# Bucketed attention with a squared-ReLU block: the operand sums of the second part are issued at other places, and three more pairs add their last key block on VectorE

## Chip, core and metric

The kernel runs on one core of one Trainium2 chip. The metric is the device time of one execution in microseconds (us). A core has TensorE (PE; its weight loads are the row PEld), VectorE (DVE), ScalarE (ACT), GpSimd (POOL) and SyncE (SP). Each of them works through its own queue of instructions in order, and SP, ACT and POOL also issue DMAs from theirs.

## What is computed

First, hash attention over 4 batches of 8 heads, with 768 positions and 64 features a head. A query sees the keys whose six sign bits under a random projection are the same as its own:

```python
q_bits = (np.einsum('bhsd,dk->bhsk', q, proj) > 0).astype(np.int64)
k_bits = (np.einsum('bhsd,dk->bhsk', k, proj) > 0).astype(np.int64)
...
mask = q_bucket[:, :, :, None] == k_bucket[:, :, None, :]
scores = np.where(mask, scale * np.matmul(q, k.transpose(0, 1, 3, 2)), -1000000000.0)
...
attn = attn / (np.sum(attn, axis=-1, keepdims=True) + 1e-09)
return np.matmul(attn, v).astype(np.float32)
```

Its output, heads side by side, is x of 3072 tokens by 512 features. The second part is `h = x @ w_in; r = np.maximum(h, 0.0); out = (r * r) @ w_out`, with w_in 512 x 2048 and w_out 2048 x 512. The two weights arrive as 64-bit floats, and the kernel makes 32-bit floats of them.

## The kernel before

**Attention** goes over 16 pairs of heads (`for pr in range(NP)`, L598), four pairs a batch. A pair has six key blocks of 128 keys. `score` (L394, L411) makes the products of a key block on PE and their exponentials on ACT (tile `e`). `attend` (L436) multiplies them by the values into `xo`. The sum of the exponentials over the keys has two steps. `add_up` (L421, L426) adds up the key blocks on DVE into the tile `total`. Then `sum_up` (L455) adds over the 128 partitions on PE, with a matmul by a matrix of ones, into the PSUM tile `tot`. In the pairs named in the dictionary `sums` (L533), `add_up` leaves the sixth key block out, and `sum_up` makes a second round of matmuls that adds it straight from `e` (L450: `srcs = [totals[pr]] + [weights[pr, SB - 1]] * (pr in sums)`). After the matmuls, DVE transposes `tot` (`flip`, L461), takes the reciprocal (`once`, L463) and writes `both` (L467). PE spreads that (`spread`, L478), and DVE normalizes (`normalize`, L488 and L494). SP stores the result to `x_all` in device memory (L498).

The order of the work is written out by hand (`tc.manual_schedule()`), and each engine gets its instructions in the order of the program. A pair's own end, `finish(pr - 1)`, is issued within the next pair, after its first two key blocks. In a pair, DVE also transposes q and k of the next pair (`features`, L331) and rounds two blocks of 64-bit weights (`part_weight`, L141 and L145; `round_weight`, L169, L174, L177). SP loads them (L128) and stores the rounded ones (L188).

**The second part** replaces eight products of blocks by seven (`product`, L697), which takes sums of the operands. It goes over 3 chunks of 1024 tokens. In a chunk, `hidden(i, r)` makes eight units of 256 hidden columns each; then `project(i)` multiplies by w_out, which is split in the same way twice. A unit of `hidden` takes the operands in this order: `x` (its four blocks b11, b12, b21 and b22 lie in one tile `x`) for two products, then `t2`, `t1`, `t3`, then `x` again, and last `t4`, which is b12 rewritten. Three pieces of work prepare this beside the attention:

- `sums_in(c)`, for each of four quarters of the columns of w_in: four DVE instructions (L508 to L511, tiles `s_in`) and eight DMAs on SP (L201) to `w_in_7`. Quarter 3 belongs to the units 6 and 7.
- `load_x(0)`, one DMA on POOL's queue (L542), and `load_unit(0)` and `load_unit(1)` on SP's (L552).
- `sums_x(0, n)`: four subtractions of 128x1024 on DVE (L514), which give t1, t3, t2 and b12 of the first chunk. For the later chunks the same four are made within `project`, after its products k = 3 and k = 4.

In the kernel before, `NIN` is 8, `PB` is 4 and `X_0` is 9. So `sums` holds the pairs 4, 5, 8 and 9 (`sums_in` of the quarters 0 to 3) and the pairs 10 and 11 (the two halves of `sums_x`). In those six pairs PE adds the last key block, and in the other ten DVE does. `load_x(0)` stands at the start of pair 9, and the two `load_unit` in pair 10. The last pair, 15, has no next pair, and so no `features`.

After the loop come `finish(15)`, `normalize(15)` and the rounding of the last block of weights; then `hidden(0, 0)` begins.

Of the kernel before, what the change touches and what calls it, by code (L numbers as in the profile page):

```python
# [34 lines left out]
def kernel(  # L35
# [22 lines left out]
    NP = B * H // 2  # L58
    PB = H // 2
# [42 lines left out]
    def turn(name):  # L102

        return ps_s.tile([P, 2, 512], FP32, name=name, tag="turn")
# [4 lines left out]
    NIN = 2 * NFT  # L109
# [267 lines left out]
    def weigh(pr):  # L377

        t = bits[pr, 1]
        nc.scalar.activation(out=t, in_=t, func=ACTF.Copy, scale=gains)  # L380
# [65 lines left out]
    def sum_up(pr, tot):  # L446


        tot = tot[:, 0]
        srcs = [totals[pr]] + [weights[pr, SB - 1]] * (pr in sums)  # L450
        for src in srcs:
            for c in range(2):
                for h in range(2):
                    g = 2 * h + c
                    nc.tensor.matmul(  # L455
                        out=tot[g * 32:(g + 1) * 32, 0:HS], lhsT=ones,
                        rhs=src[:, h, c * HS:(c + 1) * HS],
                        start=src is srcs[0], stop=src is srcs[-1],
                    )
        flip = p_n.tile([P, HS], FP32, name="flip")  # L460
        nc.vector.transpose(out=flip, in_=tot[:, 0:HS])  # L461
        once = p_n.tile([P, NB], FP32, name="once")
        nc.vector.reciprocal(  # L463
            out=once, in_=flip.rearrange("p (n f) -> p n f", f=32)[:, :, 0]
        )
        both = p_n.tile([P, 2, NB], FP32, name="both")
        nc.vector.tensor_tensor(  # L467
            out=both, in0=which,
            in1=once.rearrange("p (o n) -> p o n", o=1).to_broadcast([P, 2, NB]), op=ALU.mult,
        )  # L470
        onces[pr] = both
# [12 lines left out]
    def normalize(pr):  # L484
        b, j = divmod(pr, PB)
        rec = recs.pop(pr)
        over = p_n.tile([P, S], FP32, name="recs")
        nc.vector.transpose(  # L488
            out=over.rearrange("p (n f) -> p n f", f=32),
            in_=rec.rearrange("p (n o) -> p n o", o=1).to_broadcast([P, S // 32, 32]),  # L490
        )
        x_t = p_x.tile([P, S], FP32, name="x_t")
        xo = outs.pop(pr)
        nc.vector.scalar_tensor_tensor(  # L494
            out=x_t, in0=xo[:, 0:S], scalar=xo[:, S:S + 1],
            in1=over, op0=ALU.add, op1=ALU.mult,
        )
        nc.sync.dma_start(out=x_all[:, j, b * S:(b + 1) * S], in_=x_t)  # L498
# [14 lines left out]
    def minus(out, in0, in1):  # L513
        nc.vector.tensor_tensor(out=out, in0=in0, in1=in1, op=ALU.subtract)  # L514
# [14 lines left out]

    X_0 = 2 * PB + 1
    sums = {c // 2 * (NIN // 2) + c % 2 + NIN // 2: (sums_in, c) for c in range(4)}  # L533
    for n in range(2):
        sums[X_0 + 1 + n] = lambda n: sums_x(0, n), n

    xs = {}

    def load_x(i):

        x = p_c.tile([P, NFT, NCH], FP32, name="x")
        nc.gpsimd.dma_start(out=x, in_=x_all[:, :, i * NCH:(i + 1) * NCH])  # L542
        xs[i] = x, [p_c.tile([P, 2, NCH // 2], FP32, name=f"t_x{n}") for n in range(3)]
# [7 lines left out]
            w_unit[n] = pool.tile([P, 7, NFT // 2, P], FP32, name="w_unit", bufs=2 if pool is p_i else 1)  # L551
            nc.sync.dma_start(out=w_unit[n], in_=w_in_7[r])  # L552

    def sums_x(i, n):

        x, (t1, t2, t3) = xs[i]
        lo, hi = slice(0, NCH // 2), slice(NCH // 2, NCH)
        b11, b12, b21, b22 = x[:, 0:2, lo], x[:, 0:2, hi], x[:, 2:4, lo], x[:, 2:4, hi]
        if n == 0:
            minus(t1, b12, b11)  # L560
            minus(t3, b22, b12)
        else:
            minus(t2, b22, t1)
            minus(b12, b21, t2)

    def finish(pr, beside=None):

        tot = turn("tot")
        if beside:
            beside()  # L570
        sum_up(pr, tot)
        for kt in (SB - 2, SB - 1):
            attend(pr, kt)
        spread(pr)

    with tc.manual_schedule():
# [21 lines left out]
        for pr in range(NP):  # L598
            a, b = 2 * pr, 2 * pr + 1
            more = pr + 1 < NP  # L600

            def prepare():

                hash_bits(pr + 1, turn("hash"))
                for w in (1, 0):
                    signs(pr + 1, w)


            if pr + 2 < NP:
                load_pair(pr + 2)  # L610
            if pr == X_0:
                load_x(0)
            if more and pr > 0:
                for w in range(2):
                    features(pr + 1, w)
            if pr > 0:
                round_weight(b - 2)
                load_weight(b)
            score(pr, 0)
            if pr == 0:  # L620
                first_keys(1, turn("hash"))
            score(pr, 1)
            if pr > 0:
                finish(pr - 1, prepare if more else None)
            add_up(pr, 1)
            if pr == 0:
                for w in range(2):
                    features(1, w)
            if pr > 0:
                normalize(pr - 1)  # L630


            if pr == X_0 + 1:
                for n in range(2):
                    load_unit(n)
            part_weight(a)
            score(pr, 2)
            score(pr, 3)
            if pr == 0:
                prepare()  # L640
            elif more:
                weigh(pr + 1)
            place_power(a)
            attend(pr, 0)
            attend(pr, 1)
            for kt in (2, 3):
                add_up(pr, kt)
            if more:
                load_values(pr + 1)


            round_weight(a)
            part_weight(b)
            if more:
                load_weight(a + 2)
            score(pr, 4)
            score(pr, 5)
            if pr == 0:
                weigh(1)
            place_power(b)  # L660
            attend(pr, 2)
            attend(pr, 3)
            add_up(pr, 4)

            if pr not in sums:
                add_up(pr, 5)
            if pr in sums:
                f, n = sums[pr]
                f(n)
        finish(NP - 1)  # L670
        normalize(NP - 1)
        round_weight(2 * NP - 1)
        first.close()

# [9 lines left out]
        b11, b12, b21, b22, b_t = (  # L684
            p_g.tile([P, NR, HN], FP32, name=f"b{n}") for n in ("11", "12", "21", "22", "_t")
        )
# [196 lines left out]
        def project(i):  # L883
# [59 lines left out]
            for k in range(7):  # L943
                b = OUTER[k][1]
                t1, t2 = tens.pop(k)
                at = lambda m, k=k: lambda n: leaves[k, m][:, n]
                bt = {
                    "11": lambda n: b[:, n, 0:QN], "21": lambda n: b[:, NQ + n, 0:QN],
                    "22": lambda n: b[:, NQ + n, QN:HN], "t1": lambda n: t1[:, n],
                    "t2": lambda n: t2[:, n], "t3": lambda n: b[:, n, QN:HN],  # L950
                    "t4": lambda n: b[:, NQ + n, 0:QN],
                }

                def hook():
                    y21 = b[:, NQ:NR, 0:QN]
                    minus(y21, y21, t2)
                    if k + 1 < 7 and k not in (1, 3):
                        inner_sums(k + 1)

                counted = []  # L960

                def a_with_load(m, k=k):
                    load_leaf(7 * k + len(counted) + NLEAF - 2)
                    counted.append(m)
                    return at(m)

                use = uses[k]
                product(
                    NQ, QN, a_with_load, bt, lambda *p: use(0, *p), lambda *p: use(1, *p),
                    lambda p: use(2, p, None), lambda *p: use(3, *p), hook,  # L970
                )
                if k == 0 and i + 1 < NCHUNK:
                    load_x(i + 1)
                if k in (3, 4) and i + 1 < NCHUNK:
                    sums_x(i + 1, k - 3)
                if k == 5 and i + 1 == NCHUNK:
                    guard()
                if k == 0:

                    for h in range(2):  # L980
                        at_h = slice(h * NQ, (h + 1) * NQ)
                        minus(b11[:, at_h], b22[:, at_h], b_t[:, at_h])
                    inner_sums(2)
                if k == 2:

                    for h in range(2):
                        at_h = slice(h * NQ, (h + 1) * NQ)
                        minus(b_t[:, at_h], b21[:, at_h], b11[:, at_h])
                    inner_sums(4)
# [309 lines left out]
```

## Time and profile before

| | |
|---|---|
| median of 5 runs | 890.98 us (890.34 to 892.87) |
| the profiled execution | 891.22 us, of which the span of the profile is 889.4 us |
| busy, of the span | PE 876.3 us (99%), DVE 711.0 us (80%), ACT 376.5 us (42%), POOL 91.7 us (10%) |
| attention | to 336.4 us; the rest is the second part |
| granted clock of TensorE | 1.00 in every stage looked at |

The profile has several views. The page gives each engine's busy time, the costliest groups of instructions and, by shares, the chain of work that ended last, followed back from the last instruction. The trace answers more closely. It lists that chain piece by piece in order of time (start, length, engine, tile, line); the instructions of one engine in order of time (start, length, line, operation, output<-inputs, and in brackets how long the engine sat idle before it and what ended that); and a table of busy times by stretches of time. A group such as "L455 tot<-e x48" counts records: an fp32 matmul leaves two of them, so 48 records are 24 matmuls of six pairs.

### The profile page before, as it was taken

The page shows a single profiled execution, that of the slowest core. Times are in us where ns is not written, and L with a number is a line of the kernel's source. Part 1 is how long each engine was busy: PE and PEld are TensorE (multiplying, and loading weights), DVE is VectorE, ACT ScalarE, POOL GpSimd, SP SyncE. Part 2 cuts the span into 40 slices and gives each one's busy share as a digit, 9 for nine tenths or more (in the row PEclk, how much of TensorE's full clock was granted, in tenths as well). Part 3 has the DMA queues.
Part 4 walks back from the last instruction along what each step waited for, and adds up shares of the span by engine and source line. Part 5 has one row for each costly group of instructions (what it writes and reads, how often), then busy time and mean ns, then how long its engine had stood idle before and what let it go on. Part 6 is the DMA issues. An engine that isn't in the chain of part 4 may idle for free.

```text
span 889.4 us, 11762 instructions
## 1 busy us (share of the span) xinstructions
PE 876.3 (99%) x4292; PEld 503.2 (57%) x4292; DVE 711.0 (80%) x991; ACT 376.5 (42%) x609; POOL 91.7 (10%) x148
## 2 busy tenths in 40 slices
PE   8999999999999999999999999999999999999996
PEld 4444444444444444444688854445888644458885
DVE  5899999999999986888779955568789556778875
ACT  5988888888888851222111112222111122221110
POOL 2000000000000000554000111112000111100002
PEclk9999999999999999999999999999999999999998
DMA  9678779899976325999855743447756444444565
GB/s 186 122 150 134 196 184 191 178 276 217 266 160 148 119 90 211 292 267 286 314 174 154 190 87 125 141 154 257 253 163 171 79 154 153 150 134 144 164 174 101
DMA packets 220032, 158.14 MB, mean 178 GB/s; under 512 B 163808, under 2 KB 180704, under 8 KB 219968
## 3 DMA queue, kind: packets, MB, share of 16 engines
q1 hardware_dynamic: 186848, 84.04, 38.8%
q10 hardware_dynamic: 22384, 37.76, 13.9%
q0 software_dynamic: 10736, 35.53, 13.2%
q8 instruction: 35, 0.57, 0.3%
q14 instruction: 29, 0.24, 0.1%
HBM read 119.28 MB, written 38.01 MB: 177 GB/s over the span
## 4 chain that ended last, share of the span: by engine, by line
PE 95%; DVE 3%; ACT 1%; issue 0%; DVEq 0%
PE acc L697 59%; PE st L394 17%; PE xo L436 14%; PE tot L455 2%; PE hash L344 1%; DVE total L426 1%; ACT bits L354 1%; PE xo L324 0%; ACT e L411 0%; DVE peaks L738 0%; DVE b L787 0%; DVE h L786 0%; PE tp L307 0%; DVE t L514 0%; PE xo L478 0%
## 5 line engine op out<-in xcount | busy, mean ns | idle before, releaser
L697 PE MATMUL acc<-x,w_unit 128*128 128x512 f32 x384 | 169.3, 592 | 0.0
L411 ACT ACTIVATE e<-st 128x1024 f32<-128x1024 f32 x192 | 145.1, 810 | 48.7 <-PE st L394 44.3
L394 PE MATMUL st<-feat,feat 64*128 64x512 f32 (+1 forms) x768 | 150.4, 483 | 0.0
L436 PE MATMUL xo<-e,v_nat 128*64 128x512 f32 (+1 forms) x768 | 134.8, 492 | 0.0
L697 PE MATMUL acc<-b,leaf 128*128 128x256 f32 x600 | 132.9, 379 | 0.0
L697 PE MATMUL acc<-t_x,w_unit 128*128 128x512 f32 x288 | 127.6, 592 | 0.0
L697 PEld LDWEIGHTS acc<-x,w_unit 128*128 128x128 f32 x384 | 72.9, 190 | 90.5 <-issue 88.0
L697 PEld LDWEIGHTS acc<-b,leaf 128*128 128x128 f32 x600 | 114.0, 190 | 16.8 <-issue 1.4
L426 DVE TENSOR_TENSOR total<-total,e 128x1536 f32<-128x1536 f32 x58 | 101.9, 1757 | 3.8
L436 PEld LDWEIGHTS xo<-e,v_nat 128*64 128x64 f32 x768 | 51.4, 136 | 82.4 <-issue 75.6
L697 PEld LDWEIGHTS acc<-t_x,w_unit 128*128 128x128 f32 x288 | 54.6, 190 | 69.0 <-issue 66.7
L394 PEld LDWEIGHTS st<-feat,feat 64*128 64x128 f32 x768 | 66.0, 188 | 33.9 <-issue 24.8
L786 DVE TENSOR_TENSOR h<-acc,two 128x512 f32<-128x512 f32 x24 | 16.6, 691 | 85.2 <-PE acc L697 85.1
L704 ACT COPY two<-acc 128x512 f32<-128x512 f32 (+1 forms) x45 | 21.9, 487 | 132.6 <-PE acc L697 129.5
L697 PE MATMUL acc<-t,leaf 128*128 128x256 f32 x336 | 76.5, 380 | 0.3 <-DVE t L514 0.3
L354 ACT ACTIVATE bits<-hash,lifts 32x384 bf16<-32x384 f32 x120 | 68.8, 573 | 3.2 <-issue 1.3
L697 PEld LDWEIGHTS acc<-t,leaf 128*128 128x128 f32 x336 | 63.6, 190 | 9.8 <-DVE t L514 1.1
L704 ACT COPY one<-acc 128x512 f32<-128x512 f32 (+1 forms) x45 | 21.9, 487 | 111.0 <-PE acc L697 77.6
L787 DVE SCALAR_TENSOR_TENSOR b<-h 128x512 f32<-128x512 f32 x96 | 64.3, 690 | 2.5
L394 PE MATMUL st<-bits,bits 64*128 64x256 bf16 (+1 forms) x384 | 63.0, 325 | 1.8 <-ACT e L411 1.4
L697 PE MATMUL acc<-b_t,leaf 128*128 128x256 f32 x240 | 53.8, 379 | 0.0
L697 PEld LDWEIGHTS acc<-b_t,leaf 128*128 128x128 f32 x240 | 45.5, 190 | 6.2
(130 smaller groups left out, 870.1 us busy)
## 6 DMA issues: line engine op xcount, KB each, us to landing
leaf<-w_out ACTq DMA_DIRECT2D x142, 256.0 KB, 3.0
w_unit<-w_in SPq DMA_DIRECT2D x24, 896.0 KB, 4.7
raw<-in_moe_w_in_dram SPq DMA_DIRECT2D x16, 512.0 KB, 5.5
raw<-in_moe_w_out_dram SPq DMA_DIRECT2D x16, 512.0 KB, 4.3
w_out<-sums POOLq DMA_DIRECT2D x16, 448.0 KB, 6.8
v_nat<-in_v_dram SPq DMA_DIRECT2D x16, 384.0 KB, 4.3
x_all<-x_t SPq DMA_DIRECT2D x16, 384.0 KB, 3.1
x<-x_all POOLq DMA_DIRECT2D x3, 2048.0 KB, 11.8
```

What stands on the lines that cost most here:

```text
L344: nc.tensor.matmul(out=banks[g * NR_B:(g + 1) * NR_B, h, 0:HS], lhsT=projs[rows], rhs=feat[pr, w][rows, c * HS:(c + 1) * HS], start=True, ...
L354: nc.scalar.activation(out=t[h * D:h * D + NR_B, c * HS:(c + 1) * HS], in_=hashed[pr, w][at, h, 0:HS], func=ACTF.Sign, scale=HUGE, bias=li ...
L394: nc.tensor.matmul(out=st[:, h, 0:hi - lo], lhsT=src[pr, 1][rows, key], rhs=src[pr, 0][rows, lo:hi], start=first, stop=not first,)
L411: nc.scalar.activation(out=e[:, :, lo:hi], in_=sts[i][:, :, 0:hi - lo], func=ACTF.Exp, scale=scale)
L426: nc.vector.tensor_tensor(out=totals[pr], in0=totals[pr], in1=weights[pr, kt][:, :, 0:S], op=ALU.add)
L436: nc.tensor.matmul(out=xo[h * D:(h + 1) * D, lo:hi], lhsT=nat[pr, "v_nat"][:, h, kt * D:(kt + 1) * D], rhs=weights[pr, kt][:, h, lo:hi], s ...
L455: nc.tensor.matmul(out=tot[g * 32:(g + 1) * 32, 0:HS], lhsT=ones, rhs=src[:, h, c * HS:(c + 1) * HS], start=src is srcs[0], stop=src is sr ...
L697: nc.tensor.matmul(out=acc[to], lhsT=a(i), rhs=b(i), start=first and i == 0, stop=last and i == n - 1, skip_group_check=True,)
L704: nc.scalar.copy(out=t, in_=acc[of])
L786: nc.vector.tensor_tensor(out=h, in0=one, in1=two, op=ALU.add)
L787: nc.vector.scalar_tensor_tensor(out=out[:, r], in0=h, scalar=0.0, in1=h, op0=ALU.max, op1=ALU.mult)
```

## The change

`sums` becomes pairs 4, 5 and 8 (quarters 0, 1 and 2), so 13 pairs have their last key block added on DVE instead of ten. `X_0` becomes 12: `load_x(0)` is issued at the start of pair 12 and the two `load_unit` in pair 13. `sums_in(3)` is issued at the start of pair 15, ahead of the rounding of weights there. The four subtractions of the first chunk are single calls now, and are issued after the loop: t1 ahead of `finish(15)`, t2 and t3 within it after `sum_up`, and b12 after `normalize(15)`. Within `project` they are made in the order t1, t2, then t3, b12.

```diff
-    X_0 = 2 * PB + 1
-    sums = {c // 2 * (NIN // 2) + c % 2 + NIN // 2: (sums_in, c) for c in range(4)}
-    for n in range(2):
-        sums[X_0 + 1 + n] = lambda n: sums_x(0, n), n
+    X_0 = 3 * PB
+    sums = {NIN // 2: 0, NIN // 2 + 1: 1, NIN: 2}
...
-    def sums_x(i, n):
+    def sum_x(i, n):
...
-        if n == 0:
-            minus(t1, b12, b11)
-            minus(t3, b22, b12)
-        else:
-            minus(t2, b22, t1)
-            minus(b12, b21, t2)
+        minus(*((t1, b12, b11), (t2, b22, t1), (t3, b22, b12), (b12, b21, t2))[n - 1])
...
         sum_up(pr, tot)
+        if pr == NP - 1:
+            sum_x(0, 2)
+            sum_x(0, 3)
         for kt in (SB - 2, SB - 1):
...
                 load_x(0)
+            if not more:
+                sums_in(3)
             if more and pr > 0:
...
             if pr in sums:
-                f, n = sums[pr]
-                f(n)
+                sums_in(sums[pr])
+        sum_x(0, 1)
         finish(NP - 1)
         normalize(NP - 1)
+        sum_x(0, 4)
         round_weight(2 * NP - 1)
...
                 if k in (3, 4) and i + 1 < NCHUNK:
-                    sums_x(i + 1, k - 3)
+                    sum_x(i + 1, 2 * k - 5)
+                    sum_x(i + 1, 2 * k - 4)
```

## The prediction

> **What bounds the kernel now.** I read the page's shares first: PE is busy 99% of the span, DVE 80%. A busy PE is no proof, since its ends are modelled, so next comes the chain that ended last, piece by piece. From 30 us to the last pair it runs on PE alone, with no gap. These are pieces of it (start, length, engine, tile, line, count):
>
> ```profile
> 236.54 1.43 PE tot L455 x16
> ...
> 257.09 1.43 PE tot L455 x16
> ...
> 277.65 0.78 PE tot L455 x8
> ...
> 331.03 1.77 DVE total L426
> 332.80 0.04 issue
> 332.84 0.85 PE tot L455 x8
> 333.70 2.74 PE xo L436 x16
> 336.44 0.08 PE xo L478 x4
> ```
>
> Two things are to be seen. In pairs that stand in `sums`, the matmuls of `tot` take 1.43 us of the path, in the others 0.78. And in the last pair the chain goes over DVE: PE waits for `total`. The table of stretches, one from each `tot` to the next, gives the pitch (stretch, its length, PE busy, PEld, DVE, ACT, POOL, clock, DMA share, GB/s):
>
> ```profile
> 236.54:257.09 20.55, 20.55 (x160) 9.39 (x164) 19.07 (x23) 17.08 (x26) 0.00 (x0) 1.00 0.83 176
> 277.65:297.55 19.90, 19.90 (x152) 9.15 (x156) 18.55 (x23) 17.07 (x26) 0.00 (x0) 1.00 0.49 133
> ```
>
> PE fills both. DVE has 18.55 us of work in a pair that adds all six blocks and 19.07 in one with half of `sums_x`. Last, DVE's instructions in order of time, for the quarter sums of pair 8 and the start of pair 15:
>
> ```profile
> 190.04 0.68 DVE L508 TENSOR_TENSOR s_in<-in 128x512 f32<-128x512 f32 x1
> ...
> 192.57 0.97 DVE L331 STREAM_TRANSPOSE feat<-q_nat 128x768 f32<-128x768 f32 x1
> ...
> 313.93 0.68 DVE L169 SCALAR_TENSOR_TENSOR power<-raw,power 128x512 uint32<-128x512 uint32 x1
> 314.53 0.68 DVE L174 SCALAR_TENSOR_TENSOR top<-raw,top 128x512 f32<-128x512 uint32 x1
> 315.25 0.69 DVE L177 SCALAR_TENSOR_TENSOR out_piece<-top,power 128x512 f32<-128x512 f32 x1
> 317.50 0.58 DVE L461 STREAM_TRANSPOSE flip<-tot 128x384 f32<-128x384 f32 x1 [1.56 <-PE tot L455]
> ```
>
> Four quarter sums take 192.57 - 190.04 = 2.53 us, and in pair 15 DVE has 1.56 us free before it must transpose `tot`.
>
> **Pairs 9, 10 and 11: the second round of `tot` goes.** It costs 1.43 - 0.78 = 0.65 us of PE, which the pitches confirm (20.55 - 19.90). PE is the whole path there: 3 x 0.65 = **1.95 us less**. DVE gains three additions of 1.76 us and loses the quarter sums (2.53) and four subtractions (two take 2.27 us from start to start, 231.14 to 233.41). It ends each pair with less work than before, the work of pairs 12 and 13, which run at 19.90 with 0.65 us of DVE idle ahead of `flip`. If that cover went, PE would wait for `total`; but a plain `total` is done at 274.1 and wanted at 277.65. ACT's work is unchanged.
>
> The Trainium skill, TensorEngine Tiling (Array Packing), section Tiling Modes, says that a change of the tiling mode drains TensorE. The first round keeps that change, so the rule has the second round cost less than half, and the rows agree (0.65 against 0.78). Without it one might take half of 1.43, which would make 2.15 us of saving instead of 1.95.
>
> **`load_x`, `load_unit`.** POOL has no other work between 20 and 350 us, and `load_x(0)` sat 179 us there, until a store of pair 7's x landed. It should start as before, at 184.8 us, since it waits for data and not for its place; if it moves to pair 12 instead, its 12 us of transfer end some 50 us ahead of t1. Two `load_unit` (1.3 us of SP) move to pair 13, where SP is idle for 5 us at a time, and land about 45 us ahead of use. Both cost nothing.
>
> **Pair 15: `sums_in(3)`.** Its 2.53 us stand ahead of the weight rounding. Back to back, L177 lasts 0.61 us to the next start, so `flip` can start at 315.25 + 0.61 + 2.53 = 318.39 and not at 317.50: 0.89 us late. PE's `spread` needs `both` 0.96 us after the start of `flip`, at 319.4; it is issued at 319.79, so PE does not wait there. But from `recs` at 320.30 to the end of `total` at 332.80 DVE runs without a gap worth naming (the chain is on it), so `total` ends 0.9 us late, and PE, which waited 0.43 us for it, waits 1.3. **0.9 us more.** The ends are nothing (DVE's late start is taken up somewhere) and 2.53 (none of the idle time is usable); I take the worked value, since instruction after instruction starts back to back in that stretch.
>
> Its eight DMAs took 5.7 and 4.2 us of SP in pairs 8 and 9. In pair 15 the store of block 29 and the load of block 31 (315.97 and 316.35) queue behind them, and the load leaves by about 320.9. With the 4.3 us such a load takes it lands by 325.2, and DVE wants it at 328.5 + 0.9. Without that margin of 4 us, each us late is one on the path.
>
> **The tail.** Times are those of before, plus the 0.9 of the last pair. `total` ends at 333.7; t1 takes DVE to 334.9, `flip` follows, so `both` is there at 336.0, and PE wants it at 337.0. Then t2 and t3 (337.2 and 338.4), the two of `normalize` (340.4), b12 (341.6), and the rounding (343.6). `hidden(0, 0)` starts on PE at 337.35; a product takes 1.72 us there (four records at 0.43). So t2 is wanted at 340.9, t1 at 342.6, t3 at 344.3, b12 at 347.6: margins of 3.7 us or more, and each would cost only what it is late. Behind the later rounding stand DVE's first output of `hidden` (341.3, now 343.6), hidden by the 5.26 us for which DVE then idled, and on SP the loads of w_out rows, 2 us later against PE. Those reach DVE just as it wants them (351.8 against 351.9). If they are later, DVE slips, has 3.05 us of idle in unit 2, and PE waits for none of it. Nothing.
>
> The longer wait in the last pair leaves the clock alone if the 0.43 us of idle there, at a granted clock of 1.00, is a guide. The Trainium skill, TensorE: Matmul & The Clock Gate, Part 1, gives an idle window of about 3.4 us for the halving of the clock, and 1.3 us is under that, so by it too nothing is added; no row here shows the halving.
>
> The order within `project` changes no instruction; PE is busy throughout there. **Sum: -1.95 + 0.9 = -1.05 us.** From the profiled 891.22 that is 890.17; the median of before lies 0.24 under its profiled run, so 889.93, or **889.9 us**.
>
> **Rivals.** (1) *The whole saving stays.* The 0.9 us are absorbed in pair 15 (another of its waits gives way): 890.98 - 1.95 = 889.0. For it speaks that DVE idled 1.56 us; against it, that the chain shows DVE as last through that pair.
>
> (2) *Slower: the first product of `hidden` waits for the last write of `x`.* b12 is rewritten in the tile `x` after `normalize`, and the first matmuls of the second part read other blocks of the same tile. If waits are kept by tile, PE starts at 341.6 and not at 337.35: 4.25 us more, 890.98 - 1.05 + 4.25 = 894.2. It decides as soon as b12 ends after 337.35, so it would decide. Against it speak PE's and DVE's rows at the start of `project`:
>
> ```profile
> 432.68 1.67 PE L697 MATMUL acc<-b,leaf 128*128 128x256 f32 x7
> ...
> 435.90 0.42 DVE L514 TENSOR_TENSOR b<-b 128x256 f32<-128x256 f32 x1
> ```
>
> The DVE instruction rewrites one half of a block of b11 and stands earlier in the program; PE reads the other half 3.2 us before it runs. So waits are kept by region, there in one row of the tile, here over two rows, which the trace does not show. By the page on the clock such an idle time of over 4 us would come on top with a slower clock.
>
> (3) *Little or no gain.* DVE becomes the bound in pairs 9 to 11, or block 31 comes late by about a us: the 1.95 are eaten in part or whole, and the 0.9 stay: 890.8 to 891.9. Against it, pairs 12 and 13 already do this work at 19.90 us.
>
> **Numbers.** Forecast 58% (its own range 889.2 to 890.6), rival 1 20% (888.5 to 889.5), rival 3 12%, rival 2 10%. The range from 888.7 to 891.4 holds the forecast, most of rival 1 and over half of rival 3, some 82%. A difference of 0.2%, about what a measurement of this kernel can tell from no change, is 1.78 us: faster means under 889.2, slower over 892.8. Three quarters of rival 1 and a tenth of the forecast make faster 0.21; rival 2 and a little of rival 3 make slower 0.11; the rest is 0.68.
>
> **What would show it.** `tot` of 0.78 us and a pitch of 19.90 in the stretches after pairs 9, 10 and 11; `flip` in pair 15 without idle time before it; PE's wait for `total` at 1.3 us; the first matmul of `hidden` right behind `spread`. Wrong if PE idles anywhere between `spread` and the second unit, if DVE waits for block 31, or if `total` of pair 15 ends no later against PE than before.

## The result and the profile after

The changed kernel takes 889.43 us (median of 29 runs, 888.99 to 891.97), the kernel before 890.97 (52 runs). The ratio is 0.9983, with a 95% interval from 0.9978 to 0.9988: 1.5 us less, between 1.1 and 2.0. The forecast was 1.05 less, 889.9, and the range held the time.

The chain of work that ended last, of the changed kernel (start, length, engine, tile, line, count):

```profile
215.37 0.78 PE tot L455 x8
...
235.28 0.78 PE tot L455 x8
...
255.19 0.78 PE tot L455 x8
...
309.70 1.76 DVE total L426
311.46 0.61 DVE s_in L508
...
312.09 1.82 DMA w_in<-s_in
...
315.23 0.69 DVE out_piece L177
315.92 0.50 DVE flip L461
...
330.91 0.85 PE tot L455 x8
...
334.50 0.08 PE xo L478 x4
```

The three `tot` of pairs 9 to 11 are at 0.78. The pairs follow one another at 19.91, as the plain pairs do; the table of stretches shows it from the `tot` of `finish(10)`, and from that of `finish(12)`, to the next one:

```profile
235.28:255.19 19.91, 19.91 (x152) 9.16 (x156) 18.58 (x23) 17.07 (x26) 0.00 (x0) 1.00 0.72 157
275.10:295.00 19.90, 19.90 (x152) 9.13 (x156) 18.55 (x23) 17.07 (x26) 0.00 (x0) 1.00 0.68 218
```

The second is a stretch whose work on PE and DVE the change did not touch, and the first now looks like it, in DVE's work too (18.58 us against 18.55). The chain now leaves PE already at the end of pair 14: it is on DVE from 309.70 us (`total` of pair 14, then `s_in`) to `total` of pair 15. Before, it was on PE until 320.28 us. (One piece there is named after the store of a sum; DVE's own order in that stretch has no gap, as the next rows show.)

Two profiled runs can't simply be subtracted: already the `tot` of pair 8 starts at 194.75 us and not at 195.37. Up to there the two programs do the same work. The offset is there from the first 10 us on: PE's transposes of the first k, which in the later run wait for a load (0.39 us), start at 7.00 us before and at 6.43 now, and the first `tot` at 34.88 and 34.27. So it seems to come from the first loads, which land at another time in each run. In the experiments this `tot` starts at 194.93 to 195.33 where nothing ahead of it differs. So everything below is read from one **stretch**: from the start of the first `tot` matmul of pair 8's finish to the first matmul of `hidden`. It was 336.45 - 195.37 = 141.08 us before, and is 334.51 - 194.75 = 139.76 now, 1.32 less. From there to the end of the span it is 552.9 us in both.

The three rounds are 1.95 of it, so some 0.6 came back, in pair 15. The `tot` of `finish(14)` shows both parts, first before and then now:

```profile
316.58 0.85 PE L455 MATMUL tot<-total,ones 128*32 128x384 f32 x8
```
```profile
314.03 0.85 PE L455 MATMUL tot<-total,ones 128*32 128x384 f32 x8
```

It is 2.55 us earlier, of which 0.62 are the offset and 1.93 are saved. 1.32 are left at `hidden`, so 0.61 came back behind it. DVE there, of the changed kernel:

```profile
311.38 0.68 DVE L508 TENSOR_TENSOR s_in<-in 128x512 f32<-128x512 f32 x1
...
313.91 0.69 DVE L169 SCALAR_TENSOR_TENSOR power<-raw,power 128x512 uint32<-128x512 uint32 x1
...
315.84 0.57 DVE L461 STREAM_TRANSPOSE flip<-tot 128x384 f32<-128x384 f32 x1
...
316.81 1.75 DVE L421 SCALAR_TENSOR_TENSOR total<-e,e 128x1536 f32<-128x1536 f32 x1
318.48 0.98 DVE L488 STREAM_TRANSPOSE recs<-xo 128x768 f32<-128x768 f32 x1
...
320.77 0.42 DVE L145 TENSOR_SCALAR top<-raw 128x512 uint32<-128x512 uint32 x1
321.11 3.62 DVE L426 TENSOR_TENSOR total<-total,e 128x1536 f32<-128x1536 f32 x2
```

The same instructions of the kernel before:

```profile
318.49 1.75 DVE L421 SCALAR_TENSOR_TENSOR total<-e,e 128x1536 f32<-128x1536 f32 x1
320.30 0.98 DVE L488 STREAM_TRANSPOSE recs<-xo 128x768 f32<-128x768 f32 x1
...
322.59 0.42 DVE L145 TENSOR_SCALAR top<-raw 128x512 uint32<-128x512 uint32 x1
323.04 3.62 DVE L426 TENSOR_TENSOR total<-total,e 128x1536 f32<-128x1536 f32 x2
```

`flip` has no idle time ahead of it any more and is 0.89 us late against PE, just as worked out (317.50 - 315.84 = 1.66, where PE's `tot` is 2.55 earlier). But the steps after it are shorter. From L421 to `recs` it was 1.81 us and is 1.67; from L145 to the two additions it was 0.45 and is 0.34. Both had held a short wait, for `spread` on PE and for ACT's exponential, too short to stand as idle time in the rows of DVE. The chain of the kernel before names them, since it leaves DVE there:

```profile
320.18 0.10 PE xo L478 x4
...
320.30 0.99 DVE recs L488
...
322.41 0.60 ACT e L411
...
323.04 1.77 DVE total L426
```

In the changed kernel the chain stays on DVE at both places. The two took 0.25 of the 0.89 away, and `total` ends some 0.6 late.

PE's matmuls at the end of the attention, of the changed kernel:

```profile
330.91 0.85 PE L455 MATMUL tot<-total,ones 128*32 128x384 f32 x8 [1.04 <-DVE total L426]
...
334.33 0.26 PE L478 MATMUL xo<-both,picks 128*64 128x24 f32 x4
334.51 3.70 PE L697 MATMUL acc<-x,w_unit 128*128 128x512 f32 x8
```

The same `tot` of the kernel before:

```profile
332.84 0.85 PE L455 MATMUL tot<-total,ones 128*32 128x384 f32 x8 [0.43 <-DVE total L426]
```

PE waits 1.04 us for `total` (0.43 before), and `hidden` starts right behind `spread`, at 334.51. b12 is written by DVE at 337.10:

```profile
337.10 1.22 DVE L514 TENSOR_TENSOR x<-x,t_x 128x1024 f32<-128x1024 f32 x1
```

So the second part does not wait for the last write of the tile `x`. `load_x(0)` was issued at 184.23 us, as early as before (184.84): on POOL's queue nothing stood ahead of it, it waited for the store of its data (178.70 us), and its later place in the program changed nothing.

### The profile page after: what moved, and what is told of

It reads as the page before. It is cut to its first block, busy times and chain, and to the rows that moved or that the text cites. A ratio compares the mean times of both kernels' runs of the same rounds, so it can differ in the third digit from the quotient of the medians.

```text
span 887.4 us, 11727 instructions
## 1 busy us (share of the span) xinstructions
PE 873.6 (98%) x4268; PEld 501.7 (57%) x4268; DVE 715.9 (81%) x994; ACT 376.0 (42%) x609; POOL 91.4 (10%) x148
## 4 chain that ended last, share of the span: by engine, by line
PE 92%; DVE 4%; ACT 1%; DMA 1%; issue 1%; ACTq 0%; DVEq 0%
PE acc L697 59%; PE st L394 17%; PE xo L436 13%; PE tot L455 2%; PE hash L344 1%; DVE total L426 1%; DMA k_nat<-in_k_dram 1%; ACT e L411 1%; ACT bits L354 1%; DVE peaks L738 0%; DVE b L787 0%; DVE h L786 0%; ACTq L827 0%; DMA w_in<-s_in 0%; DVE t L514 0%
## 5 line engine op out<-in xcount | busy, mean ns | idle before, releaser
L426 DVE TENSOR_TENSOR total<-total,e 128x1536 f32<-128x1536 f32 x61 | 107.2, 1757 | 4.4
```

The source lines that it names most:

```text
L426: nc.vector.tensor_tensor(out=totals[pr], in0=totals[pr], in1=weights[pr, kt][:, :, 0:S], op=ALU.add)
```

## Experiments

**Where the saving is, and what made room for it.** Four runs. Where an edit has `rounds`, that is a list of the pairs whose last key block is added on PE; it takes the place of `sums` in `sum_up` and in the condition of `add_up(pr, 5)`.

*e1_rounds_back*, from the changed kernel:

```diff
+    rounds = 4, 5, 8, 9, 10, 11
```

> The changed kernel, with the last key block of pairs 9, 10 and 11 added by the second round of matmuls again and not by VectorE. The stretch from the start of tot in the stretch of pair 9 (the finish of pair 8) to the first matmul of hidden took 141.08 us before and 139.76 after. Theory A (the saving is the three second rounds, paid back in part in pair 15): the three tot grow from 0.78 to 1.43, the stretch is 3 x 0.65 longer, 141.7, and the time is about 1.95 us above the changed kernel, some 891.4. Theory B (the saving came from elsewhere, the earlier start or DVE's lighter pairs): the stretch stays within 0.5 us of 139.76.

The stretch is 336.88 - 195.18 = 141.70 us, as theory A had it to the last digit, and the time 891.49. The three `tot`:

```profile
215.80 1.43 PE tot L455 x16
236.36 1.43 PE tot L455 x16
256.91 1.43 PE tot L455 x16
```

So a second round costs 0.65 us of the path each time, and DVE's lighter pairs are worth nothing by themselves.

*e2_adds_only*, from the kernel before:

```diff
+    rounds = 4, 5, 8
```

> The kernel before, in which VectorE adds the last key block of pairs 9, 10 and 11 too, while the quarter sums and the sums of x stay in those pairs. Theory A (the moves are what makes room): DVE has some 19.2 us of work a pair from start to start in a pair that only adds; with 2.53 and twice 2.27 on top it is over the pitch of 19.90 by 1.8, 1.6 and 1.6 us, about 5 in all; PE's slack against DVE is 0.9 us (features of the next pair at 275.95, its hash at 276.84), so PE loses about 4 us and gains 1.95: 893 us, and the hash matmuls wait for DVE. Theory B (DVE, busy 80% of the span, has room, and the moves were not needed): 1.95 us less than before, 889.0.

893.99 us, slower than before by 0.34% (ratio 1.0034, 1.0022 to 1.0046); the stretch is 338.87 - 194.93 = 143.94, 4.8 more than what it would be without the rounds alone (139.13). Theory A holds: the three additions fit only where the sums have gone. One of PE's waits, in the pair with the quarter sums:

```profile
215.67 1.62 PE L344 MATMUL hash<-feat,projs 64*32 64x384 f32 x16 [0.92 <-DVE feat L331]
217.21 0.85 PE L455 MATMUL tot<-total,ones 128*32 128x384 f32 x8
```

The loss is larger than the 4 us expected for a reason to be seen here. In the changed kernel the hash matmuls of q and of k, both ready, take 0.88 us together:

```profile
214.50 0.88 PE L344 MATMUL hash<-feat,projs 64*32 64x384 f32 x16
```

In e2 k's feature is late, and the rows of the weight loads show that q's run first and k's after them, 1.62 us in all:

```profile
215.63 0.18 PEld L344 LDWEIGHTS hash<-feat,projs 64*32 64x32 f32 x8 [1.29 <-ACT e L411]
216.43 0.15 PEld L344 LDWEIGHTS hash<-feat,projs 64*32 64x32 f32 x8 [0.61 <-DVE feat L331]
```

`hash` took 1.62 in all three pairs. DVE, "80% busy" over the span, is nearly full in the stage that matters: 20.93 us of the 22.28 in the first of these pairs.

*e3_quarter_in_9*, from the changed kernel:

```diff
-    sums = {NIN // 2: 0, NIN // 2 + 1: 1, NIN: 2}
+    sums = {4: 0, 5: 1, 8: 2, 9: 3}
...
-            if not more:
-                sums_in(3)
```

> The changed kernel with the last quarter of the weights' sums back in pair 9, where the second round of matmuls comes back too. Theory A, by the trace: the second round costs 0.65, and pair 15 gets back the 0.63 by which it grew (the wait for total falls from 1.04 to 0.43): the stretch stays at 139.8 and the time at that of the changed kernel, 889.4. As the prediction priced it, pair 15 gives back 0.9 and the stretch is 0.25 shorter. Theory B (the quarter's DMAs or sums cost nothing in pair 15): the stretch grows by 0.65.

The stretch is 334.78 - 194.99 = 139.79, and the wait for `total` is that of before again:

```profile
331.18 0.85 PE L455 MATMUL tot<-total,ones 128*32 128x384 f32 x8 [0.43 <-DVE total L426]
```

So moving the last quarter to pair 15 bought nothing: 0.65 gained, 0.62 paid. The gain of the whole change is that of the four sums of x, 2 x 0.65 (141.08 - 139.79 = 1.29). (The time, 889.96, is 0.5 above the changed kernel's, but its ratio to before, 0.9987, has an interval from 0.9978 to 0.9997 and so holds that one's 0.9983; the medians can't tell these two apart.)

*e4_round_15*, from the changed kernel:

```diff
+    rounds = 4, 5, 8, 15
```

> The changed kernel with the second round of matmuls in pair 15 as well, where VectorE then leaves the last key block out. Theory A (PE waits 1.04 us for DVE's chain there, which gets 1.77 shorter): no wait for total, 0.65 more for the round, the stretch 0.4 us shorter, 139.4, the time 889.0. Theory B (the wait is for something else, such as ACT's last exponentials or block 31): the wait stays and the stretch grows by 0.65.

The stretch is 334.39 - 195.10 = 139.29, 0.47 less, and the time 889.19 (ratio to before 0.9976, 0.9967 to 0.9985). The chain is on PE through the end of the attention again:

```profile
330.21 1.43 PE tot L455 x16
334.46 10.96 PE acc L698 x25
```

In the last pair the round on PE is the cheaper one: VectorE is the bound there. (That is read from the trace; the medians can't tell e4 from the changed kernel.)

**The tail.** The changed kernel's trace shows something that the prediction did not have. ACT's copies and PE's weight loads in the first unit of `hidden` (in brackets the idle time and what ended it):

```profile
342.55 0.59 ACT L704 COPY five<-acc 128x512 f32<-128x512 f32 x1 [2.00 <-DMA w_out<-out_piece]
```
```profile
343.19 0.30 PEld L697 LDWEIGHTS acc<-x,w_unit 128*128 128x128 f32 x2 [0.66 <-ACT five L704]
```

`five` waits for a store to land: that of the weight block rounded last, whose memory the copy's tile now has. And PE's next product by `x` waits for `five`. It did so almost without loss, by chance of the lengths: from the first matmul of `hidden` to the second unit's first product by a `t` PE took 350.16 - 334.51 = 15.65 us, and 352.00 - 336.45 = 15.55 before. Two runs move that point; from the changed kernel, e5_tail_twice and e6_tail_behind:

```diff
         sum_x(0, 4)
+        sum_x(0, 4)
         round_weight(2 * NP - 1)
```
```diff
-        sum_x(0, 4)
         round_weight(2 * NP - 1)
+        sum_x(0, 4)
+        sum_x(0, 4)
```

> The changed kernel with the last of the four sums of x (b12) made twice, to the same values, ahead of the last rounding of weights: 1.14 us more of VectorE at that place. The prediction said that everything after spread has margins of 3.7 us or more, or ends in DVE's idle time: then nothing changes (theory B). Theory A, from the trace after: the store of the rounded block landed only at 342.5 us, and ACT's copy five, whose memory was that of the block, ended when PE's sixth product was due (343.2), so there is no margin left there and PE loses about 1.1 us in the first unit of hidden, in a gap ahead of its third group of products by x: 890.5.

> As the run before, b12 made twice, but behind the last rounding of weights. Theory A (what counts is when the rounded block is stored): five is free 1.1 us earlier than in the changed kernel, b12 is there at about 341.5 and wanted at 345, and PE loses nothing: no wait of PE's loads on five, the time that of the changed kernel, 889.4. Theory B (VectorE's length in the tail counts, wherever): 1.1 us more, as in the run before.

With the extra subtraction ahead of the rounding the time is 890.84 us, 1.4 above the changed kernel. The gap stands where theory A put it:

```profile
344.84 5.42 PE L698 MATMUL acc<-x,w_unit 128*128 128x512 f32 x12 [1.08 <-ACT five L705]
```

The 15.65 us have become 351.81 - 334.91 = 16.90.

With two subtractions behind the rounding it is 889.38, that of the changed kernel, the 15.55 us of before are back (350.63 - 335.08), and `five` follows PE directly:

```profile
342.25 0.59 ACT L705 COPY five<-acc 128x512 f32<-128x512 f32 x1 [1.13 <-PE acc L698]
```

So the tail has room for two subtractions (2.3 us) behind the rounding, and for no more than the one that is there ahead of it.

**A version that uses DVE's idle time.** A plain pair leaves DVE 0.65 us ahead of `flip`, and one of the four instructions of a quarter sum takes 0.61. *e7_one_a_pair* makes `sum_in(k)`, one of the sixteen instructions with its two stores, out of `sums_in`; from the changed kernel:

```diff
+    rounds = NP - 1,
...
-                sums_in(3)
+                for n in range(11, 16):
+                    sum_in(n)
...
-            if pr in sums:
-                sums_in(sums[pr])
+            if 4 <= pr < NP - 1:
+                sum_in(pr - 4)
```

> A version meant to beat both: the sixteen instructions of the weights' sums are given out one to a pair from pair 4 to 14 and five in pair 15, so that no pair but 15 needs the second round of matmuls. One such instruction takes 0.61 us from start to start, and VectorE idles 0.65 us ahead of flip in a pair that adds all six blocks. Theory A (that idle time can be used up): pairs 4, 5 and 8 lose 0.65 each, pair 15 ends as in the run with its round on PE (0.4 to 0.5 less than the changed kernel): 2.4 us less than it, 887.0. Theory B (a pair without idle time on VectorE falls behind, or the stores of the sums hold up others on SP's queue): waits of PE for features or total, and the time above 888.5.

893.45 us: slower than before (1.0029, 1.0016 to 1.0041). Up to the `tot` of `finish(6)` and again from that of `finish(9)` to that of `finish(13)` the pitch was 19.9, so the idle time can be used. In between, two pairs took 3.3 us more (153.73 to 196.85) and the next 0.9 (to 217.63). DVE at pair 8:

```profile
189.30 0.43 DVE L141 TENSOR_SCALAR power<-raw 128x512 uint32<-128x512 uint32 x1 [3.42 <-DMA raw<-in_moe_w_out_dram]
```

SP's queue in the same run shows why that block was late; the same loads in the changed kernel follow it, and then what SP's queue waited for in e7 between 150 and 200 us (in total, times, longest):

```profile
170.80 0.89 SPq L201 DMA_DIRECT2D w_in<-s_in  x2
171.75 2.25 SPq L285 DMA_DIRECT2D q_nat<-in_q_dram  x4
...
182.92 0.79 SPq L128 DMA_DIRECT2D raw<-in_moe_w_out_dram  x1
```
```profile
162.49 4.27 SPq L285 DMA_DIRECT2D q_nat<-in_q_dram  x4
...
176.69 0.61 SPq L128 DMA_DIRECT2D raw<-in_moe_w_out_dram  x1
```
```profile
SPq L201 <- DVE s_in L536: 23.6, 3, 9.5
```

The stores of the sum stand at a pair's end and wait there for DVE, and all loads of the next pair queue behind them, 6 to 9 us late. Two runs mend it. Both issue the stores behind the load of the next pair's second block (`put_sums`). *e9_stores_only* has that alone. *e8_stores_behind* also relieves pair 15, where six of the sixteen instructions had stood in one stretch:

```diff
-    rounds = NP - 1,
+    rounds = 4,
...
                 load_weight(b)
+                put_sums()
...
-                for n in range(11, 16):
+                for n in range(13, 16):
                     sum_in(n)
...
-            if 4 <= pr < NP - 1:
-                sum_in(pr - 4)
+            if pr == 4:
+                for n in range(4):
+                    sum_in(n)
+                put_sums()
+            if 4 < pr < 14:
+                sum_in(pr - 1)
...
-        sum_x(0, 4)
         round_weight(2 * NP - 1)
+        sum_x(0, 4)
```

> The version of one sum a pair again, mended in two places. Its trace showed the stores of the sums ahead of the next pair's loads on SP's queue, where each waits for VectorE at a pair's end: the block of weights for pair 8 came 3.4 us late. Here the stores are issued behind the load of the pair's second block. And six of the sixteen instructions had stood in one stretch ahead of flip in pair 15; now quarter 0 is made whole in pair 4, which keeps its second round, the instructions 4 to 12 go to the pairs 5 to 13, and three are left for pair 15, where VectorE adds the last block. b12 is made behind the last rounding. Theory A (VectorE's 0.65 us of idle time hold one instruction a pair, and both places were the loss): pairs 5 and 8 lose 0.65 each, flip in pair 15 is 0.3 late and not 0.9, the wait for total about 0.5 and not 1.04: the stretch from tot of pair 8's finish to hidden is 0.65 + 0.5 shorter than the changed kernel's 139.76, about 138.6, and the time 1.85 less, 887.6. Theory B (a full VectorE falls behind by itself): waits of PE for features, and no gain.

> The version of one sum a pair as it was run first, with only the place of the stores changed: behind the load of the pair's second block. Theory A (the stores held up SP's loads): VectorE does not wait for a block in pairs 8 to 10, and the hash of these pairs takes 0.81 again; the six instructions ahead of flip in pair 15 still make PE wait for both, about 0.6 us there: 3 us less than the first run of it, near 890. Theory B (the loads were late for the transfers themselves, about 300 GB/s there): DVE waits for the block as before and the time stays at 893.

e9 takes 888.16 us, 5.3 less than e7, and DVE waits for no block: the order on SP's queue was the loss, not the transfers. It was 2 us better than expected. At the first matmul of `hidden` the profiled runs are 4.15 us apart: e7 had lost a wait of 2.40 us and, in two pairs, the split of `hash` (1.62 us), which the expectation names but its 3 us do not hold in full. Another 0.3 us are in the first unit of `hidden`, where `five` waited longer in e7 (2.21 us, 1.77 in e9), and 0.8 lie further on, where no run shows the cause. e8 takes **887.78 us**, ratio to before 0.9962 (0.9949 to 0.9976), less than both kernels; its stretch is 332.86 - 194.35 = 138.51, where 138.6 was expected. (The medians of e8 and e9 can't tell these two apart.) PE waits once in it:

```profile
329.26 0.85 PE L455 MATMUL tot<-total,ones 128*32 128x384 f32 x8 [0.45 <-DVE total L426]
```

## Why the prediction was right, and where it was off

- *The second rounds, 3 x 0.65.* Right: `tot` at 0.78, pitch 19.91, and 1.94 when they are put back (e1).
- *DVE's cover in pairs 9 to 11.* Right: no wait. e2 shows that the cover is the sums' going and not a general slack.
- *Pair 15, 0.9 us.* The mechanism was right: the chain goes over DVE, and PE's wait for `total` grows. `flip` is 0.89 late, as worked out. The size at the end was off: PE's wait grew by 0.61. The step carried the 0.89 of `flip` unchanged to the end of `total`. The statement "DVE runs without a gap worth naming (the chain is on it)" hid two short waits, 0.14 ahead of `recs` and 0.11 ahead of the additions, that took a part of the delay in; the chain of before is on PE and on ACT there. With 0.61 in place of 0.9 the sum is -1.34 instead of -1.05, and the stretch has -1.32.
- *The clock.* PE's longer wait, 1.04 us, left the granted clock at 1.00 in that stretch, as the prediction had it; so did a wait of 2.40 us in e7. But "no row here shows the halving" is wrong, and the 1.00 of the table ahead holds for the stages before the end: from 870 us on the mean of the kernel before is 0.87. PE's last matmul ends at 881.7 us there and at 880.2 in the changed kernel, and the clock has fallen to one half soon after: the table of stretches has 0.50 from 885 to 886 us there and from 882 to 883 us here. PE was busy only in part just ahead of that, and no run here settles how long a wait is safe.
- *The rest.* The medians differ by 1.54, with an interval of 1.1 to 2.0. The 1.32 of the stretch lie in it, the forecast's 1.05 just outside. The 0.2 between the stretch and the medians are less than the runs can settle: e3, whose stretch is that of the changed kernel within 0.03, has a median 0.5 above it.
- *The tail costs nothing.* The result was right within 0.1 us, the reason incomplete. The sums of x were in time, as worked out. But "PE waits for none of it" was wrong of what stands behind the later rounding: its store holds memory that ACT's copy `five` needs, and PE waits for the copy. The margin was not 3.7 us, it was none, and 1.14 us more there cost 1.25 (e5: 16.90 against 15.65). That the change itself paid no more than 0.1 was luck.
- *`load_x`, block 31, the first matmul of `hidden`.* As predicted: issued at 184.23, no wait of DVE for the block, and `hidden` behind `spread`. Rival 2 fell with that: PE's first matmul by `x` is at 334.51, and DVE rewrites b12 in the same tile at 337.10, so waits are by region here also where the regions lie in two rows of one tile.
- *Rival 1*, the whole 1.95, did not happen in the stretch, but its mechanism did in part: other waits of pair 15 gave way, for 0.25 of the 0.89. The time of 889.43 lies halfway between its 889.0 and the forecast's 889.9, and in the range of each; only the trace tells them apart. *Rival 3* fell: PE's pitch in pairs 9 to 11 is that of a plain pair.

## What to carry to other kernels

Where two engines run close to each other, price a move by the place at which each of them is last, and not by busy shares. The same additions of 1.76 us were free in three pairs, cost 4.8 us together where the other sums stayed in those pairs, and in the last pair one of them was dearer than 0.65 us on PE. When an instruction is delayed, follow what it frees as well as what it makes: stores that hold memory, and a queue in order, on which one store that waits holds up every load behind it.

## What was not expected of the hardware

The hash matmuls of q and of k, which write to different partitions, ran beside each other only when both operands were ready: their sixteen records took 0.88 us together (the changed kernel) and 1.62 when the second half's operand came late (e2), so a wait of 0.9 us cost PE some 0.7 us more. And what happens in the first 10 us of a run moved the whole program by up to 0.6 us between profiled runs (the `tot` of pair 8 at 194.75 to 195.37), nearly half of what this change is worth.
